# Attention with a soft mixture of experts behind it: the last keys' products with the values in quarters of the array, and output columns in groups of 256, 128 and 128

## The chip, the core and the metric

The kernel runs on one core of a Trainium2 chip. A core has a matrix engine (TensorE; PE in the profile, PEld its weight loads), a vector engine (VectorE, DVE), a scalar engine (ScalarE, ACT), a general engine (GpSimd, POOL) and a queue engine that issues DMAs (SyncE, SP), with 16 DMA engines behind it. The metric is the device time of one execution in microseconds (us).

## The reference, cut to what matters

```
scores = q @ k.T / 8 + bias(i - j, i)           # 8 batches, 8 heads, 576 rows, head dim 64
attn   = exp(scores - max) / (sum + 1e-9)       # over the 576 keys
x      = attn @ v                               # then 4608 tokens of 512 (8 heads x 64)
logits = x @ phi                                # 32 slots = 8 experts x 4
d      = softmax of logits over the 4608 tokens # dispatch
slots  = d.T @ x                                # 32 x 512
out_e  = relu(slots_e @ w1_e) @ w2_e            # per expert: 512 -> 1024 -> 512
out    = (softmax of logits over the 32 slots) @ slot_out
```

All is float32. The bias is a small network of log distances, one value for a head, a row and a key. The weights w1 and w2 are 16.8 MB each, the output 9.4 MB.

## The kernel before, in words

**Bias.** A first stage (bias_job, 36 jobs, steps f, B, E, D) makes the bias of all heads once and writes it to DRAM; `load_bias` (L356 to L370) reads it back for two heads at a time into tiles `bm` (four) and `br`.

**Attention.** The work is cut into 32 units: four pairs of heads (hp) times eight batches (b). A unit has blocks p of 128 query rows; the rows 512 to 575 of two neighbouring units share block 4. Each block goes through these steps, named p and then the unit: S (scores, L438 and L443, two halves of 288 keys; L438 with the two heads in the upper and lower 64 rows of the array, L443, block 4, in its four quarters), t (bias and running maximum on DVE, L458), e (exponential on ACT, L467), m (DVE), n (scaling on POOL, L373), T (transposes on PE, L422), c (copy to the tile `at0` or `at1`), R and cR (the same for the last 64 keys of two blocks).

**Values.** `mix` (L529 to L557) multiplies by the values in two steps, M0 for query columns 0 to 255 and M1 for the other 320. Each has five products per head (L544), head 0 in the left 64 columns of the array, head 1 in the right 64: four of 128 keys, and a fifth of the last keys. The fifth takes all 128 rows of the array: the last 64 keys of head 0 lie in rows 0 to 63, those of head 1 in rows 64 to 127, and the values come from DRAM with 64 rows of zeros for the other head (`_apart`), so that half of what is multiplied is zero. x0 and x1 copy the results to `xts`, xs writes them to DRAM, and in the last eight units `moe` reads three pairs of heads back (fx), makes logits (L, D), exponentials and slot sums (Z), per batch.

**The order.** The table ORDER lists every step of these stages with its unit, and `then` sorts by it; a `+` sends a copy to DVE instead of ACT. Engines run their own instructions in that order and wait for each other by semaphores. SP issues its DMAs in order too: one that waits for a buffer holds up those behind it.

**Weights.** 64 tiles of 512 KB (`fetch_w`): 25 go to the pool `wp` during attention (w0, w1), 22 to buffers that the last units leave (wbm, wy, wqk and so on), and 17 follow as the first layer leaves tiles (`refetch`).

**The end.** After the table, a list written out by hand: the slots are turned, `first` (L961) multiplies by w1, `hidden` and `turn_hidden` follow, `second` (L1005) multiplies by w2 for output columns 0 to 255 (hf 0) and later 256 to 511 (hf 1), in two halves Q of the experts; `gather_slots` (L1016, L1020) adds the halves up, and `put` (L1038) makes 256 columns of one batch and sends them in one DMA of 512 KB (L1041), eight batches after hf 0 and eight after hf 1. The last 64 rows of four batches go together (L1046, L1050).

Of the kernel before, what the change touches and what calls it, by code (L numbers as in the profile page):

```python
# [13 lines left out]
ALU = mybir.AluOpType  # L14
# [14 lines left out]
f2.1/-1 B15/-1 f23.1/-1 f1.2/-1 f6.3/-1 B2/-1 E17/-1 f0.3/-1+ f20.1/-1 D10/-1 f23.2/-1 E15/-1 E2/-1 B23/-1 D5/-1
f6.2/-1 f18.1/-1 B6/-1 D17/-1 f1.0/-1+ f18.2/-1 f11.3/-1 f1.3/-1 f21.0/-1+ B1/-1 E4/-1 f18.3/-1 f18.0/-1+ D15/-1  # L30
f14.2/-1 f21.1/-1 f0.1/-1 f0.2/-1 f14.1/-1 D2/-1 f11.2/-1 E23/-1 f0.0/-1+ f11.0/-1 f11.1/-1 E1/-1 B18/-1 f9.2/-1
E18/-1 f9.3/-1+ D4/-1 f12.2/-1 f21.2/-1 f12.0/-1+ f8.0/-1 B11/-1 f12.3/-1 f9.0/-1 E6/-1 f12.1/-1 B0/-1 D7/-1 D1/-1
D23/-1 f22.2/-1 E0/-1 f26.3/-1 f14.0/-1 E11/-1 B21/-1 B12/-1 B14/-1 f31.2/-1 f8.1/-1 E21/-1 f9.1/-1 f22.0/-1 E12/-1
f20.0/-1+ f20.3/-1+ f30.1/-1 E14/-1 B9/-1 D18/-1 E9/-1 f22.3/-1 f22.1/-1 f8.2/-1 D6/-1 f25.0/-1+ f26.2/-1 f8.3/-1
f25.1/-1 S0.0/0 f31.0/-1+ f31.3/-1 B22/-1 f20.2/-1 E22/-1 B8/-1 f31.1/-1 B20/-1 D0/-1 f24.3/-1 f24.2/-1 E8/-1 D11/-1
f27.1/-1 B31/-1 f24.0/-1+ f24.1/-1 f26.1/-1 f25.3/-1 f26.0/-1+ E20/-1 f28.1/-1 f28.3/-1 f28.2/-1 D12/-1 f25.2/-1
B24/-1 D21/-1 E31/-1 D14/-1 f29.2/-1 f28.0/-1+ f30.2/-1 B26/-1 B28/-1 f29.1/-1 E24/-1 f29.3/-1 b0/-1 E26/-1 f30.0/-1
D9/-1 f29.0/-1+ f27.2/-1 f30.3/-1+ f27.3/-1 D8/-1 E28/-1 B25/-1 B29/-1 D22/-1 t0.10/0 t0.00/0 B30/-1 f32.2/-1 D20/-1
f27.0/-1+ D31/-1 f34.2/-1 E29/-1 f33.1/-1 E25/-1 E30/-1 B27/-1 b1/-1 f34.3/-1 S0.1/0 E27/-1 f34.0/-1 f34.1/-1 D26/-1
t0.11/0 f32.3/-1+ t0.01/0 S1.0/0 f32.1/-1 S1.1/0 D24/-1 D28/-1 t1.10/0 B34/-1 t1.00/0 D29/-1 f33.3/-1 D25/-1 f35.2/-1  # L40
f33.2/-1 D30/-1 f32.0/-1+ f35.3/-1 D27/-1 B32/-1 f35.1/-1 f35.0/-1+ b2/-1 S2.0/0 E34/-1 f33.0/-1+ e0.0/0 E32/-1 e0.1/0
t1.01/0 B33/-1 E33/-1 B35/-1 t1.11/0 m0/0 n0.1/0 S2.1/0 D34/-1 t2.10/0 E35/-1+ S3.0/0 t2.11/0 b3/-1 e1.0/0 e1.1/0
D32/-1 n0.0/0 T0/0 D33/-1 t2.00/0 m1/0 e2.1/0 t2.01/0 c0/0 e2.0/0 S3.1/0 t3.00/0 t3.10/0 n1.1/0 n1.0/0 t3.01/0 t3.11/0
S0.0/1 S0.1/1 R1/0 m2/0 e3.0/0 T1/0 cR1/0+ t0.00/1 D35/-1 n2.1/0 t0.10/1 t0.01/1 b4/-1 c1/0 t0.11/1 e3.1/0 S4.0/0
e0.1/1 S4.1/0 lq/2 m3/0 n2.0/0 T2/0 M0/0 e0.0/1 t4.00/0 c2/0 t4.01/0 e4.0/0 t4.10/0 m0/1 n3.0/0 n3.1/0 t4.11/0 R3/0
e4.1/0 n0.1/1 S1.0/1 x0/0 cR3/0+ t1.10/1 t1.00/1 n0.0/1 m4/0 b1/7 S1.1/1 T3/0 S2.0/1 t1.01/1 t1.11/1 S2.1/1 t2.00/1
n4.1/0 t2.10/1 n4.0/0 c3/0 S3.0/1 e1.0/1 R4/0 t2.01/1 cR4/0+ t2.11/1 T4/0 e1.1/1 c4/0 T0/1 t3.00/1 m1/1 n1.1/1 t3.10/1
S3.1/1 c0/1 e2.1/1 t3.01/1 t3.11/1 n1.0/1 e3.1/1 M1/0 R1/1 x1/0+ T1/1 e3.0/1 e2.0/1 S1.0/2 cR1/1+ S0.0/2 m3/1 m2/1
S1.1/2 c1/1 t1.10/2 S0.1/2 n3.0/1 t1.00/2 n2.1/1 t1.11/2 M0/1 n2.0/1 t1.01/2 n3.1/1 t0.10/2 t0.11/2 e1.1/2 e1.0/2
t0.00/2 m1/2 T3/1 e0.1/2 t0.01/2 x0/1+ e0.0/2 R3/1 S2.0/2 cR3/1+ S2.1/2 T2/1 lq/3 m0/2 n1.1/2 n1.0/2 n0.0/2 c3/1 T1/2  # L50
t2.10/2 t2.00/2 t2.01/2 c2/1 t2.11/2 S4.0/2 t4.00/2 n0.1/2 t4.10/2 lv/2 S4.1/2 S3.0/2 R1/2 c1/2 cR1/2 T0/2 t4.11/2
t4.01/2 S3.1/2 t3.00/2 e4.1/2 t3.10/2 xs/0 e4.0/2 t3.01/2 t3.11/2 S0.0/3 e3.0/2 S0.1/3 m4/2 e3.1/2 c0/2+ e2.0/2 e2.1/2
m3/2 M1/1 n4.1/2 t0.00/3 n4.0/2 t0.10/3 n3.1/2 t0.01/3 t0.11/3 R4/2 cR4/2 T4/2 n3.0/2 S1.0/3 m2/2 T3/2 x1/1 n2.1/2
c4/2 c3/2 S1.1/3 t1.10/3 t1.00/3 e0.1/3 lq/4 n2.0/2 S2.0/3 t1.11/3 t1.01/3 R3/2 T2/2 t2.10/3 S3.0/3 cR3/2 t2.00/3
e1.0/3 e0.0/3 t3.00/3 S3.1/3 S2.1/3 c2/2 t2.11/3 lq/5 m0/3 e1.1/3 M0/2 n0.1/3 t2.01/3 t3.10/3 t3.11/3 m1/3 t3.01/3
e2.1/3 n1.0/3 e3.0/3 M1/2 e2.0/3 n0.0/3 n1.1/3 e3.1/3 T1/3 x0/2+ x1/2 R1/3 m2/3 m3/3 cR1/3+ n2.0/3 S1.0/4 S1.1/4 c1/3
t1.10/4 n3.0/3 T0/3 n2.1/3 t1.00/4 S0.0/4 t1.11/4 t1.01/4 T2/3 c0/3 t0.10/4 n3.1/3 lv/3 xs/1 R3/3 t0.00/4 cR3/3+
S0.1/4 S3.0/4 c2/3 e1.1/4 e1.0/4 t0.11/4 t0.01/4 t3.10/4 e0.1/4 t3.00/4 S3.1/4 T3/3 S4.0/4 S4.1/4 m1/4 t4.10/4 e0.0/4
t3.11/4 c3/3 m0/4 t4.11/4 t3.01/4 t4.00/4 e3.1/4 n1.1/4 t4.01/4 M0/3 n1.0/4 n0.1/4 e3.0/4 x0/3 T1/4 n0.0/4 m3/4 R1/4
S2.0/4 cR1/4+ c1/4 S3.0/5 e4.0/4 S2.1/4 t2.10/4 t2.00/4 lv/4 S3.1/5 T0/4 t2.11/4 e4.1/4 M1/3 e2.1/4 t2.01/4 t3.00/5  # L60
m4/4 c0/4 t3.10/5 n3.0/4 n4.1/4 n4.0/4 t3.11/5 R4/4 e2.0/4 t3.01/5 T4/4 m2/4 n3.1/4 x1/3 n2.0/4 lv/6 T3/4 e3.0/5
cR4/4+ c4/4+ c3/4 lq/6 S0.0/5 S0.1/5 n2.1/4 R3/4 t0.10/5 T2/4 xs/2 e3.1/5 cR3/4 t0.00/5 t0.01/5 t0.11/5 S2.0/5 c2/4
# [162 lines left out]


@with_exitstack
def body(ctx, tc, qk, v, wcol, phi, mw1, mw2, tabh, consth, out, outr):
    nc = tc.nc
    P = 128  # L230
    S, D = 576, 64
# [63 lines left out]
    def ready():  # L295
# [6 lines left out]
        for r in range(1, 4):  # L302
            nc.gpsimd.tensor_copy(out=rsum[:, 32 * r:32 * r + 32], in_=rsum[:, 0:32])
# [844 lines left out]
```

## Time and profile before

| | us |
|---|---|
| median of three runs | 588.68 (587.24 to 593.66) |
| the profiled execution, its own time | 590.42 |
| its span, first to last instruction | 588.6 |
| PE busy in the span | 557.2 |
| DVE, ACT, POOL busy | 458.9, 456.5, 215.4 |
| bytes moved by DMA | 111.90 MB, 190 GB/s on average |

The span starts with the bias stage (to about 60 us), in which DVE and ACT are the busy engines; attention runs to about 516 us, the last batch's logits and slot sums to 530 us, and the experts and the output to the end. In a timeline the time between the starts of two rows is what the first of them cost, since the duration of a PE row holds the way through the array, which the next one overlaps. A float32 product is two PE instructions, so that x20 is ten products.

### The profile page before, as it was taken

The page shows a single profiled execution, that of the slowest core. Times are in us where ns is not written, and L with a number is a line of the kernel's source. Part 1 is how long each engine was busy: PE and PEld are TensorE (multiplying, and loading weights), DVE is VectorE, ACT ScalarE, POOL GpSimd, SP SyncE. Part 2 cuts the span into 40 slices and gives each one's busy share as a digit, 9 for nine tenths or more (in the row PEclk, how much of TensorE's full clock was granted, in tenths as well). Part 3 has the DMA queues.
Part 4 walks back from the last instruction along what each step waited for, and adds up shares of the span by engine and source line. Part 5 has one row for each costly group of instructions (what it writes and reads, how often), then busy time and mean ns, then how long its engine had stood idle before and what let it go on. Part 6 is the DMA issues. An engine that isn't in the chain of part 4 may idle for free.

```text
span 588.6 us, 18890 instructions
## 1 busy us (share of the span) xinstructions
PE 557.2 (95%) x7175; PEld 356.9 (61%) x7175; DVE 458.9 (78%) x1807; ACT 456.5 (78%) x960; POOL 215.4 (37%) x311
## 2 busy tenths in 40 slices
PE   5899999999999999999999999799999999999993
PEld 3355666767666666666666666467666666653551
DVE  8999687888798887978898889487988988652323
ACT  6999789979978898887888798578767887841233
POOL 2001444554445446444445445244335223400000
PEclk9999899999999999999999999999999999999998
DMA  5599424044927364585515434821433406499988
GB/s 187 218 334 325 128 87 129 26 134 114 301 92 271 112 214 163 199 290 215 200 51 194 148 104 158 285 69 67 146 108 127 159 21 216 139 386 402 409 359 321
DMA packets 43322, 111.90 MB, mean 190 GB/s; under 512 B 7904, under 2 KB 8032, under 8 KB 43232
## 3 DMA queue, kind: packets, MB, share of 16 engines
q1 hardware_dynamic: 43232, 110.71, 53.9%
q8 instruction: 56, 0.92, 0.6%
q14 instruction: 34, 0.28, 0.1%
HBM read 83.28 MB, written 27.41 MB: 188 GB/s over the span
## 4 chain that ended last, share of the span: by engine, by line
PE 62%; DVE 12%; ACT 8%; DMA 7%; issue 5%; SPq 2%; POOL 2%; DVEq 0%; POOLq 0%; ACTq 0%
PE ps L544 17%; PE ps L438 15%; PE ps L422 12%; DVE y L458 6%; ACT y L467 3%; PE ps L443 3%; PE ps L1005 2%; PE ps L961 2%; DMA bm<-bias_m 2%; DMA xs<-xts 2%; PE ps L886 2%; POOL y L373 2%; SPq L354 2%; ACT e L896 2%; PE ps L611 2%
## 5 line engine op out<-in xcount | busy, mean ns | idle before, releaser
L373 POOL TENSOR_SCALAR y<-y,sm 128x576 f32<-128x576 f32 x288 | 210.5, 745 | 287.8 <-DVE sm L475 172.3
L467 ACT ACTIVATE y<-y,mn 128x576 f32<-128x576 f32 x288 | 221.1, 770 | 38.9 <-DVE mn L458 31.9
L544 PE MATMUL ps<-at,v 128*64 128x256 f32 (+1 forms) x1280 | 165.6, 409 | 1.3 <-DMA v<-in_v_dram 0.7
L376 ACT COPY at<-ps 128x1024 f32<-128x1024 f32 (+2 forms) x171 | 137.2, 817 | 27.7 <-PE ps L422 22.1
L438 PE MATMUL ps<-qk 64*128 64x288 f32 x1024 | 156.3, 422 | 1.9 <-DVE mn L458 1.7
L544 PEld LDWEIGHTS ps<-at,v 128*64 128x64 f32 x1280 | 88.5, 137 | 67.4 <-DVE mn L458 7.9
L458 DVE CUSTOM_DVE_ANT_0 y<-ps,bm,mn 128x288 f32<-128x288 f32 x256 | 123.1, 511 | 6.4 <-PE ps L438 2.9
L422 PEld LDWEIGHTS ps<-ident,y 64*128 64x128 f32 x2592 | 98.8, 140 | 43.3 <-issue 18.8
L458 DVE CUSTOM_DVE_ANT_0 y<-ps,bm 128x288 f32<-128x288 f32 x256 | 107.8, 453 | 21.6 <-PE ps L438 13.6
L422 PE MATMUL ps<-ident,y 64*128 64x64 f32 x2592 | 110.8, 228 | 6.7 <-POOL y L373 4.6
L438 PEld LDWEIGHTS ps<-qk 64*128 64x128 f32 x1024 | 95.2, 189 | 23.5 <-DVE mn L458 5.0
L467 ACT ACTIVATION_READ_ACCUMULATOR y<-y,mn 128x1 f32 x288 | 54.6, 190 | 0.0
L474 DVE TENSOR_SCALAR sm<-sm 128x2 f32<-128x2 f32 x144 | 38.0, 264 | 20.9 <-ACT y L467 20.4
L458 DVE DVE_READ_ACCUMULATOR2_ANT mn<- 128x1 f32 x576 | 47.5, 83 | 0.0
L886 PE MATMUL ps<-f,wbd 128*32 128x512 f32 (+49 forms) x640 | 42.0, 400 | 5.6 <-DVE f L877 3.3
L877 DVE TENSOR_SCALAR f<-tabs,scl,nb 128x560 f32<-128x560 f32 (+17 forms) x107 | 45.2, 496 | 1.4 <-PE ps L886 0.8
L376 DVE COPY at<-ps 128x256 f32<-128x256 f32 (+2 forms) x53 | 39.4, 743 | 8.3 <-PE ps L422 6.5
L886 PEld LDWEIGHTS ps<-f,wbd 128*32 128x32 f32 x640 | 20.8, 112 | 26.8 <-issue 9.3
L475 DVE RECIPROCAL sm<-sm 128x2 f32<-128x2 f32 x144 | 23.8, 166 | 4.9
L875 ACT ACTIVATE f<-tabs,cols,scl 128x416 f32<-128x416 f32 (+17 forms) x37 | 27.0, 791 | 0.0
L896 ACT ACTIVATE e<-ps,bcon 128x591 f32<-128x591 f32 x35 | 25.1, 784 | 0.0
L443 PE MATMUL ps<-qk 64*64 64x288 f32 x256 | 23.4, 435 | 0.0
(147 smaller groups left out, 361.6 us busy)
## 6 DMA issues: line engine op xcount, KB each, us to landing
wt<-in_moe_w_dram SPq DMA_DIRECT2D x62, 512.0 KB, 8.5
qk<-in_qk_dram SPq DMA_DIRECT2D x32, 608.0 KB, 4.1
v<-in_v_dram SPq DMA_DIRECT2D x32, 320.0 KB, 4.5
bias_m<-e SPq DMA_DIRECT2D x32, 295.5 KB, 3.6
out_dram<-ob SPq DMA_DIRECT2D x16, 512.0 KB, 5.2
xs<-xts SPq DMA_DIRECT2D x24, 288.0 KB, 4.5
xo<-xs SPq DMA_DIRECT2D x8, 864.0 KB, 5.0
bm<-bias_m SPq DMA_DIRECT2D x16, 288.0 KB, 3.9
```

The source lines that it names most:

```text
L373: nc.gpsimd.tensor_scalar(out=out, in0=y, scalar1=r, scalar2=1.0, op0=ALU.mult, op1=ALU.mult)
L376: (nc.vector.tensor_copy if eng else nc.scalar.copy)(out=out, in_=in_)
L422: nc.tensor.matmul(out, src[rs], ident[rs, rs], is_transpose=True, start=True, stop=True, tile_position=(64 * r, 0))
L438: nc.tensor.matmul(pss[hh].t[:, 0:HALF], x[rs, 640 + p * P:640 + (p + 1) * P], x[rs, k0:k0 + HALF], start=True, stop=True, tile_position=( ...
L443: nc.tensor.matmul(pss[hh].t[64 * r:64 * r + 64, 0:HALF], x[rs, 1152:1216], x[rs, k0:k0 + HALF], start=True, stop=True, tile_position=(64 ...
L458: nc.vector.tensor_tensor_reduce(out=d["y", p][:, hs], in0=d["ps", p, n][hh].read()[:, 0:HALF], in1=biases[hp][p][:, hs], scale=-QS, scala ...
L467: nc.scalar.activation(out=y, in_=y, func=AF.Exp, bias=d["mn", p][:, 2 + hh:3 + hh], scale=-1.0, accum_out=d["sm", p][:, hh:hh + 1])
L474: nc.vector.tensor_scalar(out=r, in0=r, scalar1=1e-9, scalar2=None, op0=ALU.add)
L544: nc.tensor.matmul(po.t[64 * hh:64 * hh + 64, 0:w], d["v"][:, v0:v0 + 64], main[:, :, 4 * hh + i, :] if i < 4 else x[:, r0:r0 + w], start= ...
L877: nc.vector.tensor_scalar(out=f, in0=tabs[:, 0:n], scalar1=sc, scalar2=nb1[:, 0:1], op0=ALU.mult, op1=ALU.max)
L886: nc.tensor.matmul(pb.t[32 * t:32 * t + 32, a // 512, a % 512:a % 512 + c1 - c0], wbd, x, start=True, stop=True, tile_position=(0, 32 * t))
L896: nc.scalar.activation(out=e, in_=x, func=AF.Identity, bias=bcon[:, k:k + 1])
```

## The change

The fifth product of each head becomes a step of its own, Mr, after M0 and M1 (`rest`): four products of 64 keys by 64 value columns, one in each quarter of the array, two for M0's columns and two for M1's. For that M1 has its two heads swapped (o = 64 * (hh ^ c)), and what reads `xts` follows suit: logits take a second copy of phi and are cut at 256, the slot products read the other order. The values come without the zeros (576 columns instead of 640), the keys of the second head rolled by 64 instead of with 64 columns more (1152 instead of 1216), and the last keys' transposes of M0 get a tile `ar` of their own. `rsum` is 32 columns wide and applied four times.

At the end the output columns are cut in 256, 128 and 128. Batches 0 to 2 send columns 0 to 255 after the first group and 256 to 511 after the third (put_early, 512 KB each); batches 3 to 7 send columns 0 to 383 after the second group (put_wide, two DMAs of 384 KB each) and 384 to 511 after the third (put_last, two batches in a DMA of 512 KB). w2 is laid out for these groups. ORDER is another table: 2778 steps, of which 32 are the Mr, instead of 2746.

```diff
-f2.2/-1 f13.0/-1+ f13.3/-1 f3.0/-1 f10.3/-1+ f16.2/-1 f3.1/-1 f13.1/-1 f13.2/-1 f16.1/-1 f16.3/-1+ f16.0/-1+ f7.3/-1+
...
+kc01/31 cB/31 wc/31+ J8/30 F2/30 Z/31 F3/30 cC/31 d3/31 wat0/31 wqk0/31 wxo/31 zc/31 cB/30 wxk/31 cC/30"""
...
-        nc.sync.dma_start(out=phis, in_=phi.rearrange("(g p) s -> p g s", p=P))
+        nc.sync.dma_start(out=phis[:, 0], in_=phi.rearrange("(g p) s -> p g s", p=P))
+        for r in range(2):
+            nc.sync.dma_start(out=phis[64 * r:64 * r + 64, 1], in_=phi.rearrange("(g r p) s -> p r g s", r=2, p=64)[:, 1 - r])
...
-                k0 = 64 * (1 - hh) + n * HALF
+                k0 = n * HALF
...
             def keep_rest(eng):
-                o0 = (2048, 3136)[c]
-                o = target()[:, o0:o0 + 256].rearrange("a (i r n) -> a r i n", i=2, r=2)
+                if c == 0:
+                    d["ar"] = atp.tile([P, 256], F32, name="ar", tag="ar", bufs=2)
+                o = (target()[:, 3136:3392] if c else d["ar"]).rearrange("a (i r n) -> a r i n", i=2, r=2)
...
-            for i in range(5):
+            for i in range(4):
                 for hh in range(2):
-                    v0 = 64 * (4 * hh + i) if i < 4 else 512 + 64 * hh
-                    nc.tensor.matmul(po.t[64 * hh:64 * hh + 64, 0:w], d["v"][:, v0:v0 + 64],
-                                     main[:, :, 4 * hh + i, :] if i < 4 else x[:, r0:r0 + w], start=i == 0, stop=i == 4,
-                                     tile_position=(0, 64 * hh))
+                    o = 64 * (hh ^ c)
+                    nc.tensor.matmul(po.t[o:o + 64, 0:wide[c]], d["v"][:, 64 * (4 * hh + i):64 * (4 * hh + i) + 64],
+                                     main[:, :, 4 * hh + i, :], start=i == 0, stop=False, tile_position=(0, o))
+
+        def rest(_):
+            r0 = 3072 + 64 * (u % 2)
+            keys = d["ar"], source(1)[:, r0:r0 + 320]
+            for hh in range(2):
+                rs = slice(64 * hh, 64 * hh + 64)
+                for c in range(2):
+                    o = 64 * (hh ^ c)
+                    nc.tensor.matmul(d["po", c].t[o:o + 64, 0:wide[c]], d["v"][rs, 512:576],
+                                     keys[c][rs], start=False, stop=True, tile_position=(64 * hh, o))
...
+    cut0, width = (0, 256, 384), (256, 128, 128)
...
+                    if k == 0:
+                        wt = wtiles[32 + 8 * Q + 4 * fq + g][x // 2][:, 256 * (x % 2):256 * (x % 2) + 256]
+                    else:
+                        wt = wtiles[40 + 8 * k + 4 * Q + g][fq][:, P * x:P * x + P]
...
+    def put_wide(b):
+        put(b, 0, 384, lambda z: place_out(768))
...
         gather_slots(0)
-        stack(1)
-        for b in range(6):
-            put(0, b)
+        for b in range(NB):
+            put_early(b, 0)
         second(1, 0)
-        for b in range(6, 8):
-            put(0, b)
         second(1, 1)
         gather_slots(1)
-        for b in range(8):
-            put(1, b)
+        put_wide(3)
+        put_rest(0, 0)
+        put_wide(4)
+        second(2, 0)
+        put_wide(5)
+        second(2, 1)
+        put_wide(6)
+        gather_slots(2)
+        put_wide(7)
+        put_rest(0, 1)
+        for b in range(NB):
+            put_early(b, 1)
+        for q in range(2):
+            put_rest(1, q)
+        for b in range(NB, B):
+            put_last(b)
```

PE in the middle of attention, before: `ps` is a bank of PSUM, `at` holds the turned exponentials, `v` the values, `qk` keys and queries, `y` the exponentials, `ident` the identity of a transpose.

```order
L544 MATMUL ps<-at,v 64x256 x10
L443 MATMUL ps<-qk 64x288 x8
L422 MATMUL ps<-ident,y 128x64 x20
L438 MATMUL ps<-qk 128x288 x8
L422 MATMUL ps<-ident,y 128x64 x16
L544 MATMUL ps<-at,v 64x320 x10
L422 MATMUL ps<-ident,y 128x64 x34
```

The same place in the changed kernel, whose lines 547 and 557 are the products of M0 and M1 and those of Mr:

```order
L439 MATMUL ps<-qk 128x288 x8
L547 MATMUL ps<-at,v 64x320 x8
L547 MATMUL ps<-at,v 64x256 x8
L557 MATMUL ps<-ar,v 64x256
L557 MATMUL ps<-at,v 64x320
L557 MATMUL ps<-ar,v 64x256
L557 MATMUL ps<-at,v 64x320
L444 MATMUL ps<-qk 64x288 x4
L423 MATMUL ps<-ident,y 128x64 x36
```

M0 and M1 issue eight products each instead of ten, and the four of Mr stand once per unit, here between them and a block 4 that uses the quarters as well. Over the program the M steps form 47 runs before and 42 after; of the 32 Mr, 17 stand alone and 15 beside other work in quarters; and the shape into which the array is cut changes 231 times before and 253 times after, 212 and 229 of these ahead of the first product with w1.

SP's last rows, before: `ob` and `obr` are output tiles of 128 and of the last 64 rows.

```order
L857 DMA wt<-in_moe_w_dram 128x1024 x21
L1041 DMA out_dram<-ob 128x1024 x4
L1050 DMA out_dram<-obr 128x512
L1041 DMA out_dram<-ob 128x1024 x4
L1050 DMA out_dram<-obr 128x512
L1041 DMA out_dram<-ob 128x1024 x4
```

SP's last rows in the changed kernel:

```order
L882 DMA wt<-in_moe_w_dram 128x1024 x23
L1080 DMA out_dram<-ob 128x1024 x3
L1075 DMA out_dram<-ob 128x768 x2
L1105 DMA out_dram<-obr 128x768
L1075 DMA out_dram<-ob 128x768 x8
L1105 DMA out_dram<-obr 128x768
L1080 DMA out_dram<-ob 128x1024 x3
L1105 DMA out_dram<-obr 128x256 x2
L1093 DMA out_dram<-ob 128x1024 x2
L1093 DMA out_dram<-ob 128x512
```

Three outputs of 512 KB are issued ahead of the second group of columns instead of eight (six of them ahead of its first half), ten of 384 KB behind it, and what waits for the last group of columns is six outputs of 512, 256 or fewer KB and the two of `obr`.

## Rows read from the trace of the kernel before

**Rows 1.** The page: span, PE's busy time, the chain's shares by engine.

```profile
span 588.6 us, 18890 instructions
PE   557.2 (95%) x7175; PEld 356.9 (61%) x7175; DVE 458.9 (78%) x1807; ACT 456.5 (78%) x960; POOL 215.4 (37%) x311
PE 62%; DVE 12%; ACT 8%; DMA 7%; issue 5%; SPq 2%; POOL 2%; DVEq 0%; POOLq 0%; ACTq 0%
```

**Rows 2.** Busy time by stretch: attention, and its middle; columns as in the first row.

```profile
core 0: us, PE busy (x) PEld busy (x) DVE busy (x) ACT busy (x) POOL busy (x), PEclk, DMA share, GB/s
62.00:516.00 454.00, 444.53 (x5659) 298.04 (x5656) 376.93 (x1582) 377.94 (x821) 206.77 (x289) 0.99 0.46 152
100.00:300.00 200.00, 196.97 (x2466) 133.88 (x2464) 169.88 (x728) 173.60 (x373) 100.88 (x138) 1.00 0.53 177
```

**Rows 3.** Timeline of PE, products with the values: start, duration, line, tiles, shape, count.

```profile
365.69 2.91 PE L544 MATMUL ps<-at,v 128*64 128x320 f32 x20
368.54 1.34 PE L422 MATMUL ps<-ident,y 64*128 64x64 f32 x36
...
387.88 2.38 PE L544 MATMUL ps<-at,v 128*64 128x256 f32 x20
390.19 1.24 PE L438 MATMUL ps<-qk 64*128 64x288 f32 x8
...
480.98 5.07 PE L544 MATMUL ps<-at,v 128*64 128x320 f32 x40
485.98 0.71 PE L422 MATMUL ps<-ident,xo 64*128 64x64 f32 x16
```

**Rows 4.** Timeline of PE, work in quarters (L443) and in eighths (L1046).

```profile
346.98 1.27 PE L443 MATMUL ps<-qk 64*64 64x288 f32 x16
348.18 0.83 PE L422 MATMUL ps<-ident,y 64*128 64x64 f32 x20
...
559.16 0.66 PE L1046 MATMUL ps<-sst,cR 32*64 32x256 f32 x8 [0.18 <-DVE ob L376]
559.75 1.52 PE L1038 MATMUL ps<-sst,cT 32*128 32x256 f32 x16
```

**Rows 5.** Timeline of PE from 559.14 to 559.20 us: what had started by then.

```profile
559.16 0.45 PE L1046 MATMUL ps<-sst,cR 32*64 32x256 f32 x4 [0.18 <-DVE ob L376]
```

**Rows 6.** Busy time by stretch at the last change of heads, columns as in rows 2.

```profile
374.00:378.00 4.00, 3.01 (x28) 1.61 (x24) 0.96 (x5) 0.33 (x2) 0.00 (x0) 1.00 0.97 340
378.00:382.00 4.00, 1.40 (x30) 1.15 (x32) 2.10 (x11) 3.20 (x8) 1.74 (x3) 1.00 0.95 345
382.00:385.00 3.00, 3.00 (x36) 1.55 (x34) 1.97 (x8) 1.32 (x2) 2.58 (x4) 0.52 0.56 187
```

**Rows 7.** Waits from 360 to 385 us, and SP's issue of the load waited for.

```profile
DVE y L458 <- DMA bm<-bias_m: 4.5, 1, 4.5
...
369.59 1.48 SPq L354 DMA_DIRECT2D bm<-bias_m  x3
```

**Rows 8.** Busy time by stretch at the end, columns as in rows 2.

```profile
516.00:571.00 55.00, 52.39 (x687) 27.48 (x683) 20.15 (x52) 15.91 (x37) 0.00 (x0) 1.00 1.03 403
571.00:575.50 4.50, 3.59 (x40) 1.94 (x36) 1.44 (x3) 1.91 (x5) 0.00 (x0) 1.00 0.26 101
575.50:587.00 11.50, 4.52 (x56) 2.08 (x50) 3.77 (x6) 4.58 (x8) 0.00 (x0) 0.85 1.01 402
```

**Rows 9.** Timeline of PE and SP at the end.

```profile
530.46 1.07 PE L961 MATMUL ps<-wt,sT 128*32 128x512 f32 x8 [0.93 <-ACT sT L949]
...
557.67 2.89 SPq L1041 DMA_DIRECT2D out_dram<-ob  x4
...
561.32 3.66 PE L1005 MATMUL ps<-wt,hT 128*32 128x256 f32 x64
...
571.28 1.26 PE L1016 MATMUL ps<-so,sel 128*128 128x256 f32 x4
573.01 1.15 PE L1038 MATMUL ps<-sst,cT 32*128 32x256 f32 x16 [0.46 <-ACT sst L1020]
574.60 2.92 SPq L1041 DMA_DIRECT2D out_dram<-ob  x4
```

More of the change, by code (lines that the diff above doesn't have):

```diff
@@ L29 @@
[L29 to L38, printed above, removed]
@@ new lines, in rest @@
+        def rest(_):
[7 more added lines that the diff above has]
+                                     keys[c][rs], start=False, stop=True, tile_position=(64 * hh, o))
+        for c in range(2):
+            step(u, f"M{c}", lambda _, c=c: products(c))
@@ L551, in keep @@
+        step(u, "Mr", rest)
+        def keep(eng, c):
             if "xt" not in d:
                 d["xt"] = xp.tile([P, S], F32, name="xts", tag="xt", bufs=2)
-            cp(eng, d["xt"][:, 256 * c:256 * c + w], d["po", c].read()[:, 0:w])
-        step(u, f"x{c}", keep)
-        if c == 1 and hp < NP - 1:
+            cp(eng, d["xt"][:, 256 * c:256 * c + wide[c]], d["po", c].read()[:, 0:wide[c]])
+        for c in range(2):
+            step(u, f"x{c}", lambda eng, c=c: keep(eng, c))
+        if hp < NP - 1:
@@ L795, in sums @@
         def sums(_):
-            nc.tensor.matmul(m["J"].t[:, 257:258], rsum, stS2[:, 0:1], start=True, stop=True)
+            for g in range(4):
+                nc.tensor.matmul(m["J"].t[32 * g:32 * g + 32, 257:258], rsum, stS2[:, 0:1], start=True, stop=True,
+                                 tile_position=(0, 32 * g))
         def gather(_):
@@ L915, in body @@
             rows(u, p)
-        for c in range(2):
-            mix(u, c)
+        mix(u)
         if hp == NP - 1:
@@ L1034, in put, with place_out @@
+    now = []
+    def place_out(n):
+        if not now:
+            pool, tag, sizes = homes2.pop(0)
+            x = pool.tile([P, sum(sizes)], F32, name="ob", tag=tag, **({"bufs": 1} if tag == "br" else {}))
+            now.extend(x[:, sum(sizes[:i]):sum(sizes[:i + 1])] for i in range(len(sizes)))
+        x = now.pop(0)
+        return x[:, 0:n]
+    def put(b, c0, c1, ob):
+        w = c1 - c0
         for z in range(2):
@@ L1042, in put @@
-        if b % 4 == 3:
-            h = Banks(2)
-            for r in range(4):
-                rs = slice(32 * r, 32 * r + 32)
-                nc.tensor.matmul(h.t[64 * (r % 2):64 * (r % 2) + 64, r // 2, 0:256], ends["cR"][rs, b // 4, :], sst[rs],
-                                 start=True, stop=True, tile_position=(32 * r, 64 * (r % 2)))
-            obr = wp.tile([P, 2, 256], F32, name="obr", tag="w")
-            nc.scalar.copy(out=obr, in_=h.read()[:, :, 0:256])
-            nc.sync.dma_start(out=outr[b // 4, hf], in_=obr)
@@ L1069, in body @@
         hidden(1)
-        so = second(0, 0)
+        second(0, 0)
         turn_hidden(1)
```

525 lines of the change are left out of this document (279 added, 246 removed).

## The prediction

> **What bounds the kernel now.** I read the page first, then busy time by stretch, then single PE rows, and the end of the trace last. The page gives PE 95% of the span and 62% of the chain [rows 1]. The stretches say where: from 62 to 516 us, attention, PE is busy 444.5 of 454 us, and in its middle 197.0 of 200, while DVE has 85%, ACT 87%, POOL 50% and the DMA engines about half [rows 2]. The reader is to see that no other engine comes near, so time taken from PE there is time taken from the kernel, until ACT or DVE fills up. A unit takes 454 / 32 = 14.2 us. At the end it is DMA: from 516 to 571 us the DMA engines are full at 403 GB/s, then comes a hole of 4.5 us at 101 GB/s, then 11.5 us of output at 402 GB/s [rows 8]. The profiled execution took 590.42 us, 1.7 above the median of 588.68; my sum is made against it and taken off the median.
>
> **Prices of PE.** An M1 alone takes 368.54 - 365.69 = 2.85 us, an M0 alone 390.19 - 387.88 = 2.31, both joined 5.00 [rows 3]. Each has ten steps (five products, two instructions each, the two heads side by side), and they differ by 64 columns a step: 0.054 us a step, so a step of 256 columns takes 0.216 and one of 320 takes 0.270. Ten steps are 2.16 or 2.70; what is left, 0.15 us, is the price of a run: leaving one shape of the array for another and the first load of weights. Joined, 4.86 + 0.14 = 5.00, so a run pays it once.
>
> **Mr and what it replaces.** The fifth products go: two steps of 256 and two of 320 columns a unit, 0.97 us, over 32 units **31.1 us**. Mr adds four products of 64 by 64. If all four quarters run at once, it has two steps of 320 columns, 0.54 us, **17.3** in all. That quarters do run at once is seen in block 4's scores: sixteen instructions of 288 columns from 346.98 to 348.18, 1.20 us [rows 4]; four at a time are 4 x 0.243 = 0.97, two at a time would be 1.94. The 0.23 above 0.97 is the run's 0.15 and 0.08 for the second set of weights. The shape of the array changes 229 times instead of 212 ahead of the experts: 17 x 0.15 = **2.6**. Fifteen Mr stand beside other work in quarters: 15 x 0.08 = **1.2**. So 31.1 - 17.3 - 2.6 - 1.2 = **10.0 us less** on PE. Bounds: without any price for shapes the gain is 13.8; if every Mr paid for a shape before and behind it and the 0.08, 0.54 + 0.30 + 0.08 = 0.92 us a unit, it would be 31.1 - 29.4 = 1.7. I take 10, since the number of changes is counted.
>
> All of it lies on the path as long as PE bounds. With the same work in 0.31 us less a unit (200 us become 195.6) ACT rises from 87 to 89% and DVE to 87%, which still leaves PE first; x0 and x1 wait for Mr instead of M0 or M1, with a buffer of two `xts` behind them.
>
> **One thing in Mr has no row of its own.** Its products for M0 write one bank from two row halves (rows 0 to 63 into the bank's first 64 partitions, rows 64 to 127 into the other 64), and so do those for M1. Block 4's scores never do: there each half has its bank. The nearest row is L1046: four products from four strips of 32 rows, of which two and two share a bank in the same way. All four had started 0.04 us after the first [rows 5], and the eight instructions took 559.75 - 559.16 = 0.59 us [rows 4], which is two steps of 0.216 and 0.16 for the run, not four. So I take four at once, and let the other case be a rival. The Trainium skill, page "TensorEngine Tiling (Array Packing)", section "Restrictions and Gotchas" (Gotcha 1), speaks against this change: different row tiles, it says, cannot access the same PSUM bank simultaneously. By that rule Mr would have four steps instead of two; L1046 is this trace's evidence that it does not hold in this form.
>
> **The table ORDER.** It moves nearly every step, and this is where I have least to go by. What the trace shows of a bad place is the last change of heads: between 374 and 382 us PE is busy 4.4 of 8 us, and its clock is then granted at 0.52, the lower of its two levels (1.2 instead of 2.4 GHz), for 3 us [rows 6], in all about 3.6 + 3 x 0.48 = 5 us. DVE waited 4.5 us there for a tile of the bias whose load SP issued at 369.59 [rows 7]; it stands 22 steps ahead of its first use in the table, some 4 us at 80 steps a unit, so it wanted about 47 steps. In the new table that load has 59 steps of lead, but b0 at this change has 24 (33 before), and at the first change b1, b3 and b4 have 21, 27 and 7 (482, 58 and 117 before). SP may issue ahead of the table's place if nothing in front of it waits, so the lead is no wait by itself. Bounds: the 5 us go (gain 5), or two such places appear beside it (loss 10). I set the one against the other and take **nothing**, with both in the range.
>
> **The end.** Buffers come free, weights are fetched and the first layer starts (530.46 [rows 9]) about 10 us earlier, since attention ends earlier; the queue is just as full, so this shifts as a whole. In times of before: all 9.44 MB of output take 23.4 us at 403 GB/s. The hole is from 571 to 575.5 us, because the second group's output waits for `second`, `gather_slots` and the first `put` (571.28, 573.01, issue at 574.60 [rows 9]); it loses 4.5 x (1 - 101/403) = 3.4 us. The new cut has three outputs, 1.57 MB or 3.9 us, to bridge the second group instead of eight, but a second group of half the width: a `second` takes 3.66 us less half of its sixteen steps of 0.216 [rows 9], about 1.9, two of them 3.8. The three outputs are issued by about 559.6 (four take 2.89 from 557.67 [rows 9]), `second` ends near 562.8, and the first wide output follows 3.3 us later as now (571.28 to 574.60), 0.3 more for its longer copy, and 0.9 until data flows: 567.3. The weights ahead in the queue end near 571 - 11 = 560, the three outputs at 564.2: a hole of 3.1 us instead of a loss of 3.4. The wide outputs (4.7 MB, 11.7 us) then cover the third group, whose work is about as long (two `second` 3.8, five puts of 1.1, rest and gather 3). Behind it stand 3.15 MB instead of 4.72, but with DMA full throughout that changes nothing. **Gain 0.5 us**; bounds 3.4 if no hole is left, minus 4 if a second one opens.
>
> **Edits that cost nothing.** Two more loads of phi and a wider negation at the start: POOL and SP idle in the bias stage, phi is first used in the last quarter; without that cover they would cost a microsecond or two once. Loads of qk and v are 32 KB shorter each, 2.1 MB in all, while DMA is half idle. The split `rsum` products, the logits cut at 256 instead of 288 and the reversed reads keep their columns. A few copies change between ACT and DVE, which have room [rows 2].
>
> **Sum.** 10.0 + 0 + 0.5 = 10.5 us less: 579.9 in an execution like the profiled one, 588.7 - 10.5 = **578 us** as a median.
>
> **Rivals.** (1) The gain gets lost at new neighbours: places like the one at 374 us multiply, or ACT, at 89%, delays PE by a few tenths of a microsecond a unit. For it: nearly every step has other neighbours, and one late tile cost 5 us. Against it: PE's idle in the middle is 3 of 200 us, so the waits are short where loads are in time. Half to all of the gain goes: 583 to 588, **18%**. (2) **Slower**: Mr's quarters that share a bank run one after the other. Place: each Mr; price: two more steps of 0.27, 32 x 0.54 = 17.3 us, so 588.7 - 10.5 + 17.3 = 595. It decides from the point at which an Mr takes over (31.1 - 3.8) / 32 = 0.85 us, steps of 0.43 instead of 0.27. Against it is L1046 [rows 4, 5]; for it, that no product of 64 rows shares a bank in this trace. **6%**. (3) The end gives part of it back: two holes instead of one, 4 us, 582: **8%**. (4) More than forecast: the 5 us at 374 go as well, or the hole closes: 570 to 574, **10%**. The forecast itself, 575 to 582, has **55%**; 3% is for what I do not see.
>
> A measurement of this kernel can tell about 1%, 6 us, from no change. Below 582.8 lie the forecast, case 4 and half of case 3: 0.55 + 0.10 + 0.04, and half of the unseen: **0.70**. Within 1% lie case 1 and the rest of case 3: **0.22**. Slower: case 2 and the rest of the unseen: **0.08**. The range reaches from case 4's middle to most of case 1: **571 to 587**.
>
> **What would show it.** Rows of Mr: four starts within 0.03 us and two steps of 0.27 (right), or four steps (rival 2). PE busy still 98% from 100 to 300 us with units of about 13.9 us; if PE falls to 95% there, rival 1. At the changes of heads: waits of DVE for `bm` or `br`, and a granted clock near 0.5. The first product with w1 near 520 us; from there to the end 58 us as before. One hole of DMA near 555 us, and full DMA behind it; a second hole before the last outputs is rival 3. The forecast is wrong if attention does not end some 10 us earlier.

## The result, and the profile after

The changed kernel takes **581.57 us** in the median (580.36 to 582.65, four runs) against 589.47 of the kernel before (587.24 to 593.66) on the same chip: a ratio of 0.9854, 95% interval 0.982 to 0.9888, 7.9 us less. On a second chip, beside three of the experiments, it took 583.69 against 589.68, ratio 0.9895 (0.9849 to 0.9941). The profiled execution took 582.65 us.

The page of the changed kernel: the span, the engines' busy time and the chain's shares, as in [rows 1].

```profile
span 580.9 us, 19319 instructions
PE 549.4 (95%) x7367; PEld 354.8 (61%) x7367; DVE 454.4 (78%) x1811; ACT 459.2 (79%) x959; POOL 217.9 (38%) x308
PE 68%; DVE 11%; ACT 8%; DMA 6%; issue 4%; POOL 2%; SPq 0%; DVEq 0%; ACTq 0%; POOLq 0%
```

PE is busy 7.8 us less and the span is 7.7 shorter, so PE still has 95%, and more of the chain. Busy time by stretch in attention and its middle answers to [rows 2]:

```profile
core 0: us, PE busy (x) PEld busy (x) DVE busy (x) ACT busy (x) POOL busy (x), PEclk, DMA share, GB/s
62.00:506.00 444.00, 437.56 (x5750) 294.87 (x5752) 371.84 (x1597) 384.49 (x824) 208.47 (x292) 0.99 0.47 152
100.00:300.00 200.00, 197.53 (x2464) 134.98 (x2462) 165.33 (x731) 177.91 (x371) 102.22 (x141) 1.00 0.53 173
```

PE stays at 99% of the middle. ACT went from 87 to 89%, as forecast, but DVE from 85 to 83. Now one Mr, in PE's timeline (start, duration, line, tiles, shape, count):

```profile
77.16 0.98 PE L547 MATMUL ps<-at,v 128*64 128x320 f32 x6
78.06 0.43 PE L557 MATMUL ps<-ar,v 64*64 64x256 f32 x1
78.07 0.48 PE L557 MATMUL ps<-at,v 64*64 64x320 f32 x1
78.08 0.43 PE L557 MATMUL ps<-ar,v 64*64 64x256 f32 x1
78.08 0.48 PE L557 MATMUL ps<-at,v 64*64 64x320 f32 x1
78.33 0.39 PE L557 MATMUL ps<-ar,v 64*64 64x256 f32 x2
78.39 0.44 PE L557 MATMUL ps<-at,v 64*64 64x320 f32 x2
78.76 1.33 PE L423 MATMUL ps<-ident,y 64*128 64x64 f32 x36
```

Four products start within 0.02 us, two of them into each bank, and their second instructions follow 0.27 and 0.33 us behind the first start: two steps, not four. From 78.06 to 78.76 the Mr costs 0.70 us. Stretches of the changed kernel at a change of work, the way into attention and the last change of heads (columns as above):

```profile
60.00:64.00 4.00, 2.76 (x26) 1.34 (x25) 2.66 (x13) 3.65 (x9) 2.68 (x5) 0.80 0.72 204
64.00:68.00 4.00, 3.60 (x44) 2.39 (x48) 3.08 (x16) 3.35 (x7) 1.46 (x4) 0.50 0.40 111
...
362.00:392.00 30.00, 29.68 (x384) 19.97 (x382) 25.48 (x109) 26.43 (x57) 15.58 (x23) 1.00 0.44 139
```

The stall of [rows 6] is gone: in 30 us PE waits 0.3, at the full clock. On the way into attention PE pauses at 60 to 64 us, and from 64 to 68 the clock is granted at 0.50, 1.2 GHz. The kernel before has such a place too, somewhat later and smaller:

```profile
64.00:68.00 4.00, 2.89 (x17) 1.17 (x14) 2.25 (x11) 1.43 (x4) 0.45 (x2) 1.00 0.78 237
68.00:72.00 4.00, 4.00 (x32) 3.77 (x34) 3.37 (x16) 3.07 (x7) 2.52 (x4) 0.57 0.38 138
```

The end, by stretch and then by single rows of PE and SP, beside [rows 8, 9]:

```profile
550.50:554.00 3.50, 3.50 (x111) 3.14 (x104) 0.32 (x2) 0.27 (x1) 0.00 (x0) 1.00 0.99 391
554.00:557.50 3.50, 3.14 (x30) 1.25 (x30) 1.10 (x2) 1.84 (x3) 0.00 (x0) 1.00 0.08 30
557.50:577.00 19.50, 13.59 (x246) 8.70 (x244) 9.18 (x15) 7.47 (x15) 0.00 (x0) 0.93 1.00 383
```

```profile
521.33 1.92 PE L986 MATMUL ps<-wt,sT 128*32 128x512 f32 x16 [0.36 <-ACT sT L973]
...
549.73 3.70 PE L1037 MATMUL ps<-wt,hT 128*32 128x128 f32 x128
...
549.10 1.87 SPq L1080 DMA_DIRECT2D out_dram<-ob  x3
556.61 0.81 SPq L1075 DMA_DIRECT2D out_dram<-ob  x2
```

The first product with w1 comes 9.1 us earlier than in [rows 9], the first wide output is issued at 556.61 (the forecast's 567.3 for its data, less 0.9 and the shift of 10, is 556.4), and there is one hole of DMA, 3.5 us. From the first product with w1 to the end of the span it is 59.5 us, where it was 58.2.

### The profile page after: what moved, and what is told of

The parts are those of the page before. It is cut to its first block, busy times and chain, and to the rows that moved or that the text cites. A ratio compares the mean times of both kernels' runs of the same rounds, so it can differ in the third digit from the quotient of the medians.

```text
span 580.9 us, 19319 instructions
## 1 busy us (share of the span) xinstructions
PE 549.4 (95%) x7367; PEld 354.8 (61%) x7367; DVE 454.4 (78%) x1811; ACT 459.2 (79%) x959; POOL 217.9 (38%) x308
## 4 chain that ended last, share of the span: by engine, by line
PE 68%; DVE 11%; ACT 8%; DMA 6%; issue 4%; POOL 2%; SPq 0%; DVEq 0%; ACTq 0%; POOLq 0%
PE ps L439 18%; PE ps L547 16%; PE ps L423 14%; DVE y L459 6%; PE ps L911 4%; PE ps L444 3%; DMA xo<-xs 3%; ACT y L468 3%; PE ps L557 3%; PE ps L1037 2%; PE ps L986 2%; ACT f L900 2%; DMA qk<-in_qk_dram 2%; POOL y L374 2%; PE ps L1070 2%
## 5 line engine op out<-in xcount | busy, mean ns | idle before, releaser
L439 PE MATMUL ps<-qk 64*128 64x288 f32 x1024 | 161.3, 424 | 1.7 <-DMA qk<-in_qk_dram 0.9
L377 ACT COPY at<-ps 128x1024 f32<-128x1024 f32 (+2 forms) x151 | 132.1, 895 | 22.9 <-PE ps L423 18.8
L547 PE MATMUL ps<-at,v 128*64 128x320 f32 (+1 forms) x1024 | 133.7, 410 | 0.2 <-ACT y L468 0.2
L423 PE MATMUL ps<-ident,y 64*128 64x64 f32 x2592 | 113.6, 227 | 3.2 <-DVE mn L459 1.0
L439 PEld LDWEIGHTS ps<-qk 64*128 64x128 f32 x1024 | 101.3, 188 | 19.4 <-DVE mn L459 2.9
L547 PEld LDWEIGHTS ps<-at,v 128*64 128x64 f32 x1024 | 69.9, 137 | 54.5 <-DVE mn L459 6.5
L911 PE MATMUL ps<-f,wbd 128*32 128x79 f32 (+44 forms) x640 | 44.1, 403 | 6.6 <-DVE f L902 3.9
L377 DVE COPY at<-ps 128x1024 f32<-128x1024 f32 (+2 forms) x41 | 31.2, 763 | 5.4 <-PE ps L423 4.4
L900 ACT ACTIVATE f<-tabs,cols,scl 128x432 f32<-128x432 f32 (+15 forms) x38 | 26.4, 748 | 2.4 <-DMA bias_m<-e 2.4
L557 PE MATMUL ps<-at,v 64*64 64x320 f32 x128 | 23.9, 448 | 0.0
```

The source lines that it names most:

```text
L377: (nc.vector.tensor_copy if eng else nc.scalar.copy)(out=out, in_=in_)
L423: nc.tensor.matmul(out, src[rs], ident[rs, rs], is_transpose=True, start=True, stop=True, tile_position=(64 * r, 0))
L439: nc.tensor.matmul(pss[hh].t[:, 0:HALF], x[rs, S + p * P:S + (p + 1) * P], x[rs, k0:k0 + HALF], start=True, stop=True, tile_position=(64 * ...
L547: nc.tensor.matmul(po.t[o:o + 64, 0:wide[c]], d["v"][:, 64 * (4 * hh + i):64 * (4 * hh + i) + 64], main[:, :, 4 * hh + i, :], start=i == 0 ...
L557: nc.tensor.matmul(d["po", c].t[o:o + 64, 0:wide[c]], d["v"][rs, 512:576], keys[c][rs], start=False, stop=True, tile_position=(64 * hh, o))
L900: nc.scalar.activation(out=f, in_=tabs[:, 0:n], func=AF.Relu, bias=cols[:, 1:2], scale=sc)
```

## The experiments

All times are medians. The kernel before took 589.56 us beside the first four kernels, 589.68 beside the next four, 591.87 beside the last four; the ratios are to it.

**1 and 2. The two ends, exchanged.** `old_end` is the changed kernel with the end of before (its core below), `new_end` the reverse:

```diff
-    cut0, width = (0, 256, 384), (256, 128, 128)
-    def second(k, Q):
+    def second(hf, Q):
...
-    def put(b, c0, c1, ob):
+    def put(hf, b):
```

> The changed attention (table, Mr, values without zeros) with the old end, two groups of 256 output columns. Theory: the new cut of the output columns did not give the 0.5 us forecast but cost about 1.3 us, since the stretch from the first product with w1 to the end is 58.2 us in the kernel before and 59.5 us in the changed one; then this kernel is 1.3 us faster than the changed one, about 580.3 us, with 58.2 us in that stretch. Rival: the new cut gives 0.5 us as forecast and the 1.3 us come from what attention hands over (weights that stand later in the queue); then this kernel is 0.5 us slower than the changed one, about 582, with about 60 us in that stretch. Both: attention ends 9 to 11 us earlier than in the kernel before.

> The attention of before with the new end, output columns in groups of 256, 128 and 128. Theory (the cut costs about 1.3 us): 1.3 us slower than before, with 59.5 us from the first product with w1 to the end. Rival (the cut gives 0.5 us): 0.5 us faster than before, with 57.7 us in that stretch. Attention as before under both: last product with the values near 516.4 us in the trace.

`old_end`: 583.44 us, ratio 0.9901 (0.9867 to 0.9934), 59.3 us from the first product with w1 to the end. `new_end`: 591.07, ratio 1.0037 (1.0006 to 1.0069), 59.0 us. Neither side has it: behind the attention of before the new cut costs 0.8 us of that stretch, behind the changed attention 0.2, and the changed attention costs 1.1 us of it with the old end and 0.5 with the new one (one trace each). As a whole `new_end` is 2.2 us slower than before (0.4 to 4.1). Since the medians of `old_end` and the changed kernel came from different chips, the pair was run once more (9 and 10).

**3. Mr in two rounds instead of one.**

```diff
-                    o = 64 * (hh ^ c)
+                    o = 64 * hh
```

> The changed kernel with the heads of M1 not swapped, so that the two products of a head in Mr fall into the same quarter of the array and run one after the other: two steps of 256 and two of 320 columns instead of two of 320. The shapes of the array, the table, the copies and the DMAs stay. (The two heads of the last 320 columns of a unit arrive swapped at the logits and the slots, so only its time is read.) Theory, PE bounds attention: Mr takes 0.97 instead of 0.54 us, 0.43 more in each of 32 units, 13.8 us, so about 595 us, slower than before. Rival: in the changed kernel ACT and waits at new neighbours bound attention, and PE's time is partly hidden: less than 8 us more, under 590.

592.41 us, ratio 1.0047 (1.002 to 1.0074): about 10 us more than the changed kernel, between the two. In its timeline the same Mr as above:

```profile
77.94 0.65 PE L557 MATMUL ps<-ar,v 64*64 64x256 f32 x4
78.43 0.70 PE L557 MATMUL ps<-at,v 64*64 64x320 f32 x4
79.06 1.33 PE L423 MATMUL ps<-ident,y 64*128 64x64 f32 x36
```

It takes 1.12 us instead of 0.70, as expected, and all 32 take 31.6 instead of 20.8. But by the end of the last unit's Mr the kernel is only 8.3 us behind the changed one; it falls back by 0.26 us a unit, evenly. So each microsecond that PE is spared here had given back about 0.8. The rest of the 10 us is lost behind attention: in this trace the clock is low during the first products with w1, and the first 96 instructions take 12.38 us instead of 10.51.

```profile
530.00:535.00 5.00, 4.77 (x28) 1.22 (x32) 0.94 (x6) 0.17 (x1) 0.00 (x0) 0.59 1.04 401
```

**4. The bias loads earlier, in the kernel before.** Three steps of its table move:

```diff
-... t1.01/24 b0/23 n3.1/23 ... T1/23 b4/23 n2.1/23 ... R3/23 b3/23 x1/22 ...
+... b1/23 b0/23 t2.00/23 ... b3/23 e3.1/23 ... n1.1/23 b4/23 x0/22+ ...
```

> The kernel before with three bias loads of the last change of heads (b0, b3 and b4 of unit 23) moved to earlier places in the table, so that the load that was waited for has 56 steps of lead instead of 22; nothing else changes. Theory: the stall at 374 to 385 us in the kernel before is this load coming late, and it was worth 5 to 6 us, so this kernel takes about 584 us and shows no granted clock near 0.5 there; part of the changed kernel's gain is then this place in its new table. Rival: the load waits for a buffer or a filled queue and not for its place, so moving it gives under 1 us and the stall stays.

587.12 us, ratio 0.996 (0.993 to 0.9991), with a lead of 62 steps by the table: 2.4 us less, half of what the idle time and the clock in [rows 6] add up to. The stretches of [rows 6] in this kernel:

```profile
378.00:382.00 4.00, 4.00 (x68) 2.65 (x68) 1.54 (x8) 3.31 (x9) 2.91 (x4) 1.00 1.03 401
382.00:385.00 3.00, 3.00 (x53) 2.24 (x51) 2.68 (x13) 2.42 (x4) 1.47 (x2) 1.00 0.88 275
```

The stall and the low clock are gone, so the late load was the cause. What the place itself gave is seen in the two rows of [rows 3] that stand around it, here in this kernel:

```profile
368.79 2.91 PE L543 MATMUL ps<-at,v 128*64 128x320 f32 x20
385.85 2.38 PE L543 MATMUL ps<-at,v 128*64 128x256 f32 x20 [0.43 <-DVE mn L457]
```

They came at 365.69 and 387.88 before. So this execution is 3.1 us late ahead of the place and 2.0 early behind it: the place gave 5.1 us, as much as its idle time and its clock add up to. The 3.1 us were lost by 69 us, long ahead of the moved loads; why is not shown. In `new_end`, which has the attention of before with its late load, the same two rows stand 19.47 us apart instead of 22.19, and the clock stays at 1.00 from 374 to 390 us:

```profile
378.00:382.00 4.00, 1.83 (x42) 1.45 (x44) 1.71 (x9) 3.59 (x9) 2.13 (x3) 1.00 1.04 400
```

So the stall does not cost the same in each execution: by these three traces its removal gives 5.1 us against one and 2.4 against the other, and 2.4 (0.5 to 4.1) is the difference of the medians.

**5. The new table alone**: the kernel before, its products and its end, in the changed order.

```diff
-f2.2/-1 f13.0/-1+ f13.3/-1 f3.0/-1 f10.3/-1+ f16.2/-1 f3.1/-1
+f6.1/-1 f7.0/-1 f8.3/-1 f15.0/-1+ f12.3/-1 f15.1/-1 f15.3/-1+
...
```

> The kernel before (its products with zeros for the other head, its end) in the order of the changed table, without the Mr steps; one step, M1 of unit 14, stands 2 places later than in that table, since its fifth product needs a copy that stands behind it. It tells apart what the table gives and what the quarters give. Theory (forecast: the table gives nothing, the quarters all): 588 to 591 us, within 1.5 of before; the last change of heads shows no granted clock near 0.5, the beginning loses 1 to 2 us more than before. Rival 1 (the table gives a good part of the 7.9 us): 585 or less. Rival 2 (the new order costs, and the quarters gave more than they seem to): 593 or more.

595.3 us, ratio 1.0093 (1.0065 to 1.012): **5.5 us slower** than before, rival 2. The last change of heads is clean here too, so the table costs elsewhere what it saves there, and more. Its profiled execution was its fastest (591.70 us) and shows 1.3 us over before's, with no stall in attention but the one at 60 to 64 us. Its loss shows when the same work is compared: 18 units, from the last M products of unit 2 to those of unit 20, in the kernel before, in this one and in the changed one (columns as above):

```profile
102.32:338.22 235.90, 232.43 (x2902) 157.48 (x2898) 202.25 (x859) 203.16 (x436) 118.74 (x163) 1.00 0.51 171
103.15:344.02 240.87, 237.65 (x2901) 161.86 (x2898) 195.79 (x864) 208.35 (x436) 119.43 (x164) 1.00 0.49 161
102.70:337.06 234.36, 231.76 (x2901) 158.76 (x2898) 194.79 (x861) 207.89 (x435) 118.48 (x163) 1.00 0.49 161
```

The new order takes 5.0 us longer for the same instructions, and PE is busy in all of it. Counted from start to start, the scores and transposes take 4.6 us more, the products with the values 0.4. Over units 21 to 24, with the last change of heads, it then takes 4.3 us less (57.95 to 53.62). Why scores and transposes cost more in this order was not taken apart; where the other 3.6 us of a usual run lie, no trace shows.

**6. Without Mr.**

```diff
         def rest(_):
-            ... the four products ...
+            pass
```

> The changed kernel without the products of Mr (the last keys' products with the values are left out, so the output lacks them); table, copies, transposes and DMAs stay. Takes 20.8 us from PE, what the 32 Mr of the changed kernel's trace take from their start to the next start. Theory: attention is still bound by PE and gives back about three quarters of what PE is spared (8.3 of 10.8 us in the run with two rounds), so 14 to 17 us less than the changed kernel, about 567. Rival: at 98.5% PE is already at the point where ACT, DVE and POOL set the pace; under 8 us less, 575 or more.

**7. Exponentials without their sums.**

```diff
-                nc.scalar.activation(out=y, in_=y, ..., scale=-1.0, accum_out=d["sm", p][:, hh:hh + 1])
+                nc.scalar.activation(out=y, in_=y, ..., scale=-1.0)
```

> The changed kernel with exponentials that leave out the sums (the second instruction of each, 0.19 us x 256 = 49 us of ACT; the scaling uses another value, so the output is not the reference's). Theory: the PE time that does not arrive (a quarter of what it is spared, 0.1 to 0.2 us a unit) is lost in waits on ACT, which is busy 88% in attention; with 1.5 us a unit less on ACT these waits go and the kernel gets 3 to 6 us faster than the changed one. Rival: ACT is not what PE waits for; under 1.5 us.

**8. A shorter pause on the way into attention.**

```diff
+                for n in range(4 if (u, p, kk) == (0, 0, 3) else 1):
+                    for k in range(2 if n else 1):
                         for r in range(2):
-                            half_turn(pt.t[:, r, 64 * kk:64 * kk + 64], y[:, k0:k0 + P], r)
+                            half_turn(pt.t[:, r, 64 * (kk - k):64 * (kk - k) + 64], y[:, k0 - P * k:k0 - P * k + P], r)
```

> The changed kernel with 12 transposes of the first block issued again, 1.06 us of PE in a place where PE waits 1.0 us (at 61.3 us), so that its pause between the bias stage and attention is shorter. Theory: the clock of about 0.5 for 5 us behind that pause (64 to 69 us), which costs 2.5 us and which the kernel before has less of, comes from the pause, and goes or shrinks; 1 to 2.5 us faster than the changed kernel. Rival: the other pauses of that stretch are enough for the clock to fall; 0 to 1 us slower.

These three ran together. `turns_again`: 582.86 us, ratio 0.9861 (0.9825 to 0.9898). The 12 transposes took 0.37 us, not 1.06, so most of the pause stayed, and so did the low clock, 0.59 from 64 to 68 us. It tells nothing of a filled pause, but being the changed kernel otherwise it is the measure for the other two. `no_rest`: 579.59, ratio 0.9804 (0.9761 to 0.9848), **3.3 us less for 20.8 us of PE**: the rival. `no_sums`: 578.97, ratio 0.9793 (0.9743 to 0.9844), 3.9 us less: the theory's time, but its edit does two things. ACT's busy time falls by 22 us (459.2 to 436.8), not by 49; and the sums on DVE no longer wait for the exponentials, for which they waited 17.4 us between 100 and 500 us in the changed kernel. Which of the two gave the 3.9 us was not separated. The middle of attention in `no_rest`, then in `no_sums`:

```profile
100.00:300.00 200.00, 191.37 (x2362) 130.88 (x2358) 166.63 (x737) 177.98 (x373) 103.90 (x142) 1.00 0.53 174
```

```profile
100.00:300.00 200.00, 198.59 (x2495) 137.09 (x2495) 167.05 (x739) 168.19 (x236) 103.03 (x142) 1.00 0.53 174
```

Without Mr PE falls to 95.7%, while ACT stays at 89%: PE waits. What it waits for most is the scaling on POOL, which follows the exponentials and the sums; from 100 to 500 us (in all, times, longest), in the changed kernel and then in `no_rest`:

```profile
PE ps L423 <- POOL y L374: 0.8, 4, 0.3
PE ps L423 <- POOL y L374: 7.0, 19, 0.8
```

Without the sums ACT falls to 84% and PE rises to 99.3%. So the changed kernel stands where PE's bound meets that of the chain exponential, sums, scaling: 10.8 us more on PE cost 8.3 in attention (experiment 3), 20.8 us less give 3.3. That ACT's load and not the waits along the chain is the second bound was not shown. (PE's busy time falls by 14.8 us in `no_rest`, 549.4 to 534.6, and not by 20.8: other rows take longer there.)

**9 to 11. Both ends once more, on one chip, and five early batches instead of three** (the diff is of the last).

```diff
-    NB = 3
+    NB = 5
```

> The same kernel as in the run of this name before, beside the changed kernel on the same chip. In the traces the stretch from the first product with w1 to the end is 59.3 us with the old end and 59.5 with the new one behind the same attention, 58.2 and 59.0 behind the attention of before. Theory: the new cut of columns gives or takes less than 1 us, and most of the 1.3 us lost in that stretch comes from attention; so within 1 us of the changed kernel. Rival (by the medians of different chips, 583.4 against 581.6): 1.5 to 2.5 us slower than the changed kernel, so the new cut does gain.

> The changed kernel once more, beside the three others on the same chip. Both theories: a ratio to before between 0.982 and 0.989.

> The changed kernel with five batches instead of three that send 256 columns at once, and three instead of five that send 384. Theory: the hole of the DMA queues ahead of the first wide output shrinks, since two more outputs of 512 KB (1.05 MB, 2.6 us at 403 GB/s) bridge it while PE comes 2 x 0.73 = 1.5 us later to the second group; with three wide batches instead of five behind it the outputs of the third group are then short by about as much. So 0 to 1.5 us faster than the changed kernel. Rival: what is lost in the end is not that hole but the rate at which PE makes outputs behind it; then it is 1 us or more slower, with a second hole near the third group.

`old_end_again`: 582.98 us, ratio 0.9886 (0.9846 to 0.9926); the changed kernel, `after_again`: 583.69, 0.9895 (0.9849 to 0.9941); `five_early`: 583.75, 0.9884 (0.9843 to 0.9925). The three cannot be told apart, so behind the changed attention the new cut of the columns gives and takes nothing that a run shows. The second run of the changed kernel lies a little above the ratio that was expected of it. In the traces the stretch from w1 to the end is 59.1, 59.5 and 58.7 us: five early batches save 0.8 us there.

**12. A short third group.**

```diff
-        for fq in range(2):
-            for x in range(4):
+        for fq in range(2 if k < 2 else 1):
+            for x in range(4 if k < 2 else 1):
```

> The changed kernel with an eighth of the third group's products with w2 (so 128 output columns are not the reference's): the two second of that group take 0.3 instead of 1.7 us each. Theory: in the end the rate at which PE makes outputs behind the first wide one sets the time, and the stretch from the first product with w1 to the end falls from 59.5 by 1.5 to 2.8 us. Rival: the DMA queue sets it, and the stretch falls by less than 0.7 us.

One execution: 581.11 us, and 58.7 us in the stretch, 0.9 less; between the two. One of PE's two rows of the third group, each 1.95 us in the changed kernel:

```profile
556.81 0.42 PE L1037 MATMUL ps<-wt,hT 128*32 128x128 f32 x8
```

About 3 us are taken from PE between the wide outputs and 0.9 arrive. By this one execution PE's rate sets a part of the end; that the queue sets the rest is likely, not shown.

## Why the prediction was right, point by point

**The time** was forecast at 578 us and came at 581.57: in the range, in the case that had the most weight, near its upper edge. The gain was 7.9 us instead of 10.5, and 6.0 on the second chip.

**PE's 10.0 us: right.** The forecast price of the 32 Mr, with shapes and neighbours, was 17.3 + 2.6 + 1.2 = 21.1 us; from each Mr's start to the next start they take 20.8 in the trace. That leaves 31.1 - 20.8 = 10.3. `table_only` and `old_end`, which have the same order and the same end, differ by 10.5 us of PE's busy time (558.9 and 548.4); from before to `old_end` it falls by 8.8 (557.2), since the new order takes some of it. The first product with w1 came at 521.33, 9.1 us earlier.

**Rival 2 fell**, as the row that the prediction had set against it said: in 31 of the 32 Mr four starts within 0.02 us, in the other within 0.15; 0.70 us for an Mr alone. The Trainium skill, page "TensorEngine Tiling (Array Packing)", section "Restrictions and Gotchas" (Gotcha 1), says that different row tiles cannot access one PSUM bank at once; two row tiles that write different partitions of one bank do so here in every Mr. What the rival would have cost is seen in experiment 3, which has the four steps for another reason: 592.4, where the rival said 595.

**"All of it lies on the path as long as PE bounds": right, and only just.** The prediction named ACT at 89% as what would come next. The next bound is nearer than I thought: with 20.8 us more off PE only 3.3 would have come (experiment 6). A microsecond of PE is worth 0.8 above this point (experiment 3, 8.3 of 10.8) and 0.16 below it (3.3 of 20.8). The sign set for it, units of 13.9 us instead of 14.2, did not come: those were means over all of attention, and in the 18 units compared in experiment 5 a unit went from 13.1 to 13.0 us. The quarters' gain, 0.31 us a unit by the forecast, is nearly used up there by what the new order costs.

**The table at nothing: the step that failed.** With the products of before the new order costs 5.5 us (experiment 5), inside the bound of 10. The prediction looked for its price in late loads and the pauses behind them, two more such places at the worst. The trace shows the price on PE itself: 5.0 us in 18 units, in which PE is busy for all of them and pauses no more than before, against a saving of 4.3 at the last change of heads. Of the 5 us set for that stall, the traces of experiment 4 show 5.1 against the execution that the forecast was read from, 1.7 us above the median and with the clock low behind the stall, and 2.4 against one in which the clock stayed high. The changed kernel has both: it takes 1.5 us less than before in those 18 units, where 0.31 us a unit would be 5.6, and 6.1 less in units 21 to 24 (57.95 to 51.85). The way into attention, which looks worse in its trace, has cost that trace 0.4 us by the end of unit 2 (102.32 to 102.70).

In the same table the quarters are worth more than 10 by the medians: from `table_only` to the changed kernel the ratio is 0.9895 / 1.0093 = 0.980, some 11.6 us, end included. The intervals of the two ratios are wide enough for 10. Experiment 3, with the last keys in a step of their own but in two rounds, is 2.9 us faster than `table_only` on another chip, in spite of 12 more changes of shape (229 and 217 ahead of the first product with w1) and with as much time on PE for the products with the values (162.5 and 162.3 us); their intervals touch, so a part may be the place of the last keys, or their loads without zeros, but that is not shown.

**The end at 0.5 us less: a size below what runs can tell.** By the forecast's own terms, a hole of 3.1 us for a loss of 3.4, it was 0.3. The hole came where it was forecast, 3.5 us long. The stretch to the end of the span became 1.3 us longer, not shorter: 0.5 to 1.1 of it came with the changed attention, 0.2 to 0.8 is the new cut. The new order is not the cause, since `table_only` has 58.2 us there with the old end; what else in the changed attention is, was not found. The medians of both ends are the same behind the changed attention.

So the sum came within 2.6 us on the first chip and 4.5 on the second by other terms: there -11.6 and +5.5, for -6.0 in all, in place of -10, 0 and -0.5. That the time still fell into the forecast's own case is in part luck: the table's 5.5 us alone would have put 578 at 583.5, outside it.

## What to carry to other kernels

An engine at 99% of a stretch tells what bounds it, not how far. Here the next engine had 88 to 89%, and a gain of 2% on the first used up most of what was there. Leaving out work, whatever the output, finds that point in one or two runs; but an edit that also unties a wait, like the one of experiment 7, does not say which engine the next bound is.

The idle time and the low clock of a stall are what its removal gives against that one execution. Here the same place cost 2.7 us less in another, and the medians gave half of the sum.

An order that is written anew has a price of its own. It can be measured by running the old work in it, and it need not show as waits: compare the time that the same units take, since PE was at 99% in both orders and yet 5 us slower in one.

## What the runs showed of the hardware

Products in two row halves of the array that write the two partition halves of one bank ran at once in every Mr of the changed kernel's trace: 0.02 us between the first and the fourth start in 31 of 32, and in the one shown 0.27 us from the first start to the second instructions of 256 columns and 0.33 to those of 320.

On the way into attention all eleven traces of kernels with the new table show a low granted clock from 64 to 68 us, 0.50 to 0.60 in ten and 0.69 in `table_only`, behind 4 us in which PE was busy for 1.8 to 2.8 us; 0.37 us of work put into that pause left it at 0.59. The kernel before shows 0.57 from 68 to 72 us, behind 4 us with 2.9 busy.
